# A fused attention, expert and gated feed-forward kernel: ScalarE makes the upper parts of all expert weights from block 6 on, and the experts' results are turned later

## The chip, the cores and the metric

The kernel runs on one core of a Trainium2 chip. The metric is the device time of one execution in microseconds (us). One execution was also taken with the hardware profiler; its rows are quoted below.

## The reference, cut to what matters

```python
# attention: 16 heads of 768 positions, 64 wide; a query sees the keys of its own hash bucket
scores = np.where(mask, scale * np.matmul(q, k.transpose(0, 1, 3, 2)), -1e9)
x = softmax(scores) @ v                      # as 1536 tokens x 512
# experts: 8, each token goes to one of them
h = np.maximum(xe @ w1[e], 0.0)              # w1[e]: 512 x 1024
out[mask] = gate_w[mask, None] * (h @ w2[e]) # w2[e]: 1024 x 512
# gated feed-forward on all 1536 tokens
xn = x / rms * rms_g
g = xn @ w_gate                              # 512 x 1536
return silu(g) * (xn @ w_val) @ w_out        # w_out: 1536 x 512
```

Everything is float32. The last layer's weights and scale arrive as 64-bit floats.

## The kernel before, in words

TensorE (PE) multiplies in its float32 matmul format, so every operand is held as two parts: `hi`, the value rounded to that format, and `lo`, the rest. A product is three matmuls: hi by hi, hi by lo and lo by hi. Three stages follow each other: attention (to about 265 us), the experts (265 to 453 us) and the gated feed-forward (453 us to the end). The order of each engine's instructions is written by hand, and every engine works through its own list in that order.

**Experts.** An expert has eight weight blocks of 128 x 1024, four of `w1` and four of `w2`; block `i` of the whole stage belongs to expert `i // 8`. Expert `e` runs four inner steps `f` over `w1` (24 matmuls into `ph`, then ScalarE's Relu to `hh` and VectorE's remainder `hl`) and four steps over `w2` (12 wider matmuls into the two banks `py`). At the head of each step `convert(i)` prepares a block that TensorE needs four steps later. The preparation has three parts:

- SP's queue loads the block into one of five `raw` tiles (L256).
- `split_piece` first calls `finish_split`, which issues the pass of VectorE (DVE) that makes `lo` of the block split before (L288) and then the load that reuses its `raw` tile. Then it issues the copy that makes `hi` of the new block: on GpSimd (POOL) for even blocks (L287), on ScalarE (ACT) for odd ones (L285).
- Six half blocks of the last layer's weights are converted in between by `split_half` (L325 to L334).

Blocks 0 to 5 are split during attention, on GpSimd alone. `flip_window(e + 1)` turns the next expert's tokens on TensorE in two groups of transposes. While expert `e` runs its first steps, `finish_rows` of expert `e - 1` scales its result on ScalarE and DVE (`y`, L205), and GpSimd scatters it to the memory table `yd` with two indirect transfers (L168).

**Hand-over.** The gated feed-forward needs all 1536 tokens as 12 turned tiles, four to a group `b`. `load_y(tt)` loads one from `yd` on SP's queue (L1132), into one of three buffers. `flip_y` makes four transposes into one of two PSUM banks `f`, copies the token numbers (`ids`) and `hi` (`gxh`, L1148) on ScalarE and makes `lo` (`gxl`, L1149) on DVE; then it asks for the tile three further on. `fillers` is a list of such generators, and `fill_pe` takes one step from it after each step of an expert. Before the change three loads stand at the end of the first product of expert 6, tiles 0 to 7 are turned after the eight steps of expert 7, and tiles 8 to 11 inside `glu(0, 1)`. A load of tiles 0 to 7 is declared free of the scatters of experts 6 and 7, but waits for those of experts 0 to 5; a load of tiles 8 to 11 waits for all.

**Gated feed-forward.** `glu(p_, b)` makes four groups of 12 matmuls (`pg`, `pv` twice), `project(p_, b)` four groups of six. Their order is glu(0,0), glu(0,1), project(0,0), glu(0,2), project(0,1) and so on.

Of the kernel before, what the change touches and what calls it, by code (L numbers as in the profile page):

```python
# [44 lines left out]
def turns(t):  # L45

    return t.rearrange("p (h a) -> p a h", h=2)
# [26 lines left out]
def lsh_attention_moe_glu(  # L74
# [15 lines left out]
    nc = tc.nc  # L90
# [185 lines left out]
    def split_piece():  # L276

        finish_split()
        i = at["piece"]
        at["piece"] += 1  # L280
        new_part(i, first[i][1], ring)
        hi, lo = parts[i][2:]
        r = raws.pop(0)
        if i % 2:
            nc.scalar.copy(hi, r)  # L285
        else:
            nc.gpsimd.tensor_scalar(hi, r, 1.0, 0.0, ALU.mult, ALU.add)  # L287
        pending.append((i, lambda: (nc.vector.tensor_tensor(lo, r, hi.bitcast(F32), ALU.subtract), load_next())))  # L288

    def split_early():  # L290
# [865 lines left out]
    with ExitStack() as mc:  # L1156
# [52 lines left out]
                    split_half()  # L1209

        done = iter(())
        for e in range(E):
            xh, xl = xT.pop(e)
            hid = []
            for f in range(NF):
                i = e * 2 * NF + f
                convert(i)
                wh, wl = part(i)[0:2]
                ph = ps_h.tile([P, 2, W], F32, tag="h", name=f"ph{e}{f}")
                for s_ in range(2):  # L1220
                    fs = slice(s_ * P, (s_ + 1) * P)
                    for c in range(KC):
                        nc.tensor.matmul(ph[:, s_], wh[:, c, fs], turns(xh[:, c]), start=c == 0, stop=False)  # L1223
                        nc.tensor.matmul(ph[:, s_], wh[:, c, fs], turns(xl[:, c]), start=False, stop=False)  # L1224
                        nc.tensor.matmul(ph[:, s_], wl[:, c, fs], turns(xh[:, c]), start=False, stop=c == KC - 1)  # L1225
                parts.pop(i)
                hh = mp.tile([P, 2, W], F32R, tag="hh", name=f"hh{e}{f}", bufs=6)
                hl = mp.tile([P, 2, W], F32R, tag="hl", name=f"hl{e}{f}", bufs=6)
                nc.scalar.activation(hh, ph, AF.Relu)
                nc.vector.scalar_tensor_tensor(hl, ph, 0.0, hh.bitcast(F32), ALU.max, ALU.subtract)  # L1230
                hid.append((hh, hl))
                next(done, None)
                if e == E - 2 and f == NF - 1:

                    for tt in range(YB):
                        load_y(tt)
                if f == (F0 if e == 0 else 1):
                    fillers.append(flip_window(e + 1))
                fill_pe()
            py = [ps_y.tile([P, DM], F32, tag="y", name=f"py{e}{j}") for j in range(2)]  # L1240
            for f in range(NF):
                i = e * 2 * NF + NF + f
                convert(i)
                wh, wl = part(i)[0:2]
                hh, hl = hid[f]
                for s_ in range(2):
                    fc = 2 * f + s_
                    for j in range(2):
                        js = slice(j * P, (j + 1) * P)
                        nc.tensor.matmul(py[j], hh[:, s_, js], turns(wh[:, s_]), start=fc == 0, stop=False)  # L1250
                        nc.tensor.matmul(py[j], hh[:, s_, js], turns(wl[:, s_]), start=False, stop=False)
                        nc.tensor.matmul(py[j], hl[:, s_, js], turns(wh[:, s_]), start=False, stop=fc == 2 * NF - 1)
                parts.pop(i)
                fill_pe()
            if e == E - 1:
                for f_ in fillers:
                    for _ in f_:
                        pass
            if e == E - 2:
                fillers.append(flip_y(0, (NBLK - 1) * TB))  # L1260
            done = finish(e, py)
        for _ in done:
            pass
        for tt in range((NBLK - 1) * TB, min(NT, (NBLK - 1) * TB + YB)):
            load_y(tt)


    with ExitStack() as gc:
# [9 lines left out]
        NP = F2 // W  # L1278
        freed = N1 + EARLY

        def glu(p_, b, filler):
            gh, gl = part(N1 + 3 * p_)[0:2]
            vh, vl = part(N1 + 3 * p_ + 1)[0:2]
            hi = rp.tile([P, 2, CW], F32R, tag="y2", name=f"hi{p_}{b}")
            lo = gp.tile([P, 2, CW], F32R, tag="lo2", name=f"lo{p_}{b}")
            for s_ in range(2):
                if p_ > 0 or b in GLU0:
                    split_half(freed + DEPTH)
                fs = slice(s_ * P, (s_ + 1) * P)
                pg = ps_g.tile([P, CW], F32, tag="g", name=f"pg{p_}{b}{s_}")  # L1290
                pv = ps_v.tile([P, CW], F32, tag="v", name=f"pv{p_}{b}{s_}")
                for ps_, wh, wl in ((pg, gh, gl), (pv, vh, vl)):
                    for c in range(KC):
                        nc.tensor.matmul(ps_, wh[:, c, fs], turns(xTh[b][:, c]), start=c == 0, stop=False)  # L1294
                        nc.tensor.matmul(ps_, wh[:, c, fs], turns(xTl[b][:, c]), start=False, stop=False)  # L1295
                        nc.tensor.matmul(ps_, wl[:, c, fs], turns(xTh[b][:, c]), start=False, stop=c == KC - 1)  # L1296
                sg = gp.tile([P, CW], F32, tag="sg", name=f"sg{p_}{b}{s_}")
                nc.scalar.activation(sg, pg, AF.Silu)
                nc.vector.tensor_tensor(sg, pv, sg, ALU.mult)  # L1299
                nc.scalar.copy(hi[:, s_], sg)  # L1300
                nc.vector.tensor_tensor(lo[:, s_], sg, hi[:, s_].bitcast(F32), ALU.subtract)
                for _ in range(2):
                    next(filler, None)
            hid[p_, b] = (hi, lo)

        def project(p_, b):
            oh_, ol_ = part(N1 + 3 * p_ + 2)[0:2]
            hi, lo = hid.pop((p_, b))
            for i in range(TB):
                tt = b * TB + i  # L1310
                ts_ = slice(i * P, (i + 1) * P)
                if i % 2 and p_ + b > 0:
                    z = ps_x.tile([P, DM], F32, tag="wx", name=f"z{p_}{tt}")
                else:
                    z = ps_z.tile([P, DM], F32, tag="z", name=f"z{p_}{tt}")
# [11 lines left out]
        last = None  # L1327
        for p_ in range(NP):
            for b in range(NBLK):
                filler = iter(())  # L1330
                if p_ == 0 and b == NBLK - 2:
                    filler = flip_y((NBLK - 1) * TB, NT)
                glu(p_, b, filler)
                for _ in filler:
                    pass
                if last is not None:
                    project(*last)
                    if last[1] == NBLK - 1:
                        for j in range(3):
                            parts.pop(N1 + 3 * last[0] + j)  # L1340
                        freed = max(N1 + EARLY, N1 + 3 * (last[0] + 1))
                last = (p_, b)
# [30 lines left out]
```

## Time and profile before

| what | value |
|---|---|
| time, median of 3 runs | 744.7 us (743.47 to 746.56) |
| the profiled execution: its time | 744.9 us |
| its span from first to last instruction | 742.9 us |
| TensorE busy | 720.8 us (97%) |
| VectorE (DVE) busy | 594.6 us (80%) |
| ScalarE (ACT) busy | 375.0 us (50%) |
| GpSimd (POOL) busy | 254.6 us (34%) |
| granted TensorE clock over the span | 0.998 |

A busy share is a mean over stages with different limits. TensorE's 97% means that its idle time is only some 22 us in all, so what counts is where these lie. A matmul's busy time contains its latency, so time that TensorE lost is also read from how far apart matmuls start.

### The profile page before, as it was taken

Reading aid. Unit: us, or ns where it says so; the run is one execution under the profiler, and the core shown is the slowest. Engines: PE = TensorE matmul, PEld = TensorE weight load, DVE = VectorE, ACT = ScalarE, POOL = GpSimd, SP = SyncE. Lnnn points to the kernel's source line nnn. Section 1 sums busy time; section 2 is a strip of 40 time slices with the busy share of each in tenths; the row PEclk is TensorE's granted clock in tenths of the full one; section 3 lists DMA queues with packets and bytes.
Section 4 is the critical chain, followed back from the end, with each engine's and each line's share of the span. In section 5 each row is a group of like instructions: output and inputs, shape, how many; then the busy total and the mean of one; then the engine's idle time right before and its main releaser. Section 6 shows DMA issues by size and latency. Waiting matters only on the chain.

```text
span 742.9 us, 12599 instructions
## 1 busy us (share of the span) xinstructions
PE 720.8 (97%) x4459; PEld 653.4 (88%) x4460; DVE 594.6 (80%) x1094; ACT 375.0 (50%) x777; POOL 254.6 (34%) x434
## 2 busy tenths in 40 slices
PE   8999999999999899999989999999999999999996
PEld 6898999999999899998989888888888888888885
DVE  5999999999999757888789967855877878778533
ACT  4898989998989535335453354433221221212210
POOL 4243344347645523325244333121121121211124
PEclk9999999999999999999999999999999999999999
DMA  6799956566651156777778585321122122210012
GB/s 164 175 250 249 235 138 158 140 153 176 175 129 37 51 176 203 232 213 242 246 219 263 151 288 160 117 86 58 56 80 63 56 82 62 69 45 1 0 58 113
DMA packets 80820, 103.45 MB, mean 139 GB/s; under 512 B 32072, under 2 KB 50504, under 8 KB 80753
## 3 DMA queue, kind: packets, MB, share of 16 engines
q1 hardware_dynamic: 76752, 92.95, 44.4%
q0 software_dynamic: 3200, 9.46, 3.4%
q8 instruction: 36, 0.59, 0.3%
q14 instruction: 32, 0.25, 0.1%
q10 hardware_dynamic: 800, 0.20, 0.1%
HBM read 69.53 MB, written 14.72 MB: 113 GB/s over the span
## 4 chain that ended last, share of the span: by engine, by line
PE 63%; DVE 15%; DMA 8%; issue 5%; ACT 4%; POOL 3%; SPq 2%; POOLq 0%; DVEq 0%; ACTq 0%
PE T L607 7%; DVE lo L288 5%; PE z L1317 4%; PE z L1319 4%; PE z L1318 4%; PE pv L1295 4%; PE pg L1295 4%; PE pg L1296 4%; PE pv L1296 4%; PE pg L1294 4%; PE pv L1294 4%; PE S L569 3%; PE O L639 3%; PE S L570 3%; PE O L641 3%
## 5 line engine op out<-in xcount | busy, mean ns | idle before, releaser
L333 POOL TENSOR_TENSOR wa<-wa,hi 128x512 f32<-128x512 f32 x36 | 58.1, 1613 | 215.9 <-ACT hi L329 209.5
L329 ACT CAST hi<-wa 128x512 fp32r<-128x512 f32 x36 | 22.3, 621 | 161.7 <-DVE wa L327 154.7
L588 ACT ACTIVATE P<-S,negm 128x768 f32<-128x768 f32 x96 | 95.8, 998 | 10.4 <-DVE negm L579 6.3
L617 DVE TENSOR_TENSOR ptl<-T,pth 128x384 fp32r<-128x384 f32 x192 | 97.3, 547 | 1.5 <-ACT pth L616 0.8
L574 DVE TENSOR_REDUCE neg<-S 128x1 f32<-128x768 f32 x96 | 90.8, 946 | 2.9 <-PE S L570 2.4
L616 ACT CAST pth<-T 128x384 fp32r<-128x384 f32 x192 | 83.2, 488 | 3.0 <-PE T L607 2.2
L288 DVE TENSOR_TENSOR lo<-raw,hi 128x1024 fp32r<-128x1024 f32 x58 | 83.3, 1470 | 1.6 <-POOL hi L287 1.6
L607 PE MATMUL T<-ident,P 128*128 128x128 f32 x576 | 81.5, 275 | 0.9 <-DVE ptl L617 0.5
L607 PEld LDWEIGHTS T<-ident,P 128*128 128x128 f32 x576 | 67.8, 141 | 7.0 <-DVE ptl L617 3.2
L569 PE MATMUL S<-kA,qA 76*128 76x384 f32 x192 | 66.2, 345 | 1.8 <-ACT P L588 0.9
L1225 PE MATMUL ph<-xTh,lo 128*128 128x256 f32 x224 | 61.7, 275 | 2.1 <-DVE lo L288 2.1
L570 PE MATMUL S<-kB,qB 128*128 128x384 f32 x192 | 63.0, 328 | 0.6 <-DMA qB<-kql 0.6
L1223 PE MATMUL ph<-xTh,hi 128*128 128x256 f32 x224 | 62.8, 280 | 0.0
L1224 PE MATMUL ph<-xTl,hi 128*128 128x256 f32 x224 | 61.6, 275 | 0.0
L639 PE MATMUL O<-ptl,vst 128*64 128x384 f32 (+1 forms) x198 | 59.8, 332 | 0.0
L1299 DVE TENSOR_TENSOR sg<-pv,sg 128x512 f32<-128x512 f32 x36 | 24.7, 687 | 40.9 <-PE pv L1296 40.9
L1294 PE MATMUL pg<-gxh,hi 128*128 128x512 f32 x144 | 54.7, 380 | 0.0
L1317 PE MATMUL z<-hi,hi 128*128 128x512 f32 x144 | 54.7, 380 | 0.0
L1295 PE MATMUL pg<-gxl,hi 128*128 128x512 f32 x144 | 54.6, 379 | 0.0
L1296 PE MATMUL pg<-gxh,lo 128*128 128x512 f32 x144 | 54.6, 379 | 0.0
L1294 PE MATMUL pv<-gxh,hi 128*128 128x512 f32 x144 | 54.6, 379 | 0.0
L1295 PE MATMUL pv<-gxl,hi 128*128 128x512 f32 x144 | 54.6, 379 | 0.0
(236 smaller groups left out, 1953.3 us busy)
## 6 DMA issues: line engine op xcount, KB each, us to landing
raw<-in_moe_w_dram SPq DMA_DIRECT2D x64, 512.0 KB
raw<-in_moe_w_gate_dram SPq DMA_DIRECT2D x12, 512.0 KB
raw<-in_moe_w_val_dram SPq DMA_DIRECT2D x12, 512.0 KB
raw<-in_moe_w_out_dram SPq DMA_DIRECT2D x12, 512.0 KB
xs<-fill SPq DMA_DIRECT2D x16, 257.0 KB
xw<-xs SPq DMA_DIRECT2D x7, 514.0 KB
yt<-yd SPq DMA_DIRECT2D x12, 256.5 KB
v<-in_v_dram SPq DMA_DIRECT2D x16, 192.0 KB
```

The lines of the kernel that those rows point to most:

```text
L288: pending.append((i, lambda: (nc.vector.tensor_tensor(lo, r, hi.bitcast(F32), ALU.subtract), load_next())))
L569: nc.tensor.matmul(s_[:, j, 0:HW], qA[n][:, t * P:(t + 1) * P], turns_by_tile(kA[n][:, cs]), start=True, stop=False)
L570: nc.tensor.matmul(s_[:, j, 0:HW], qB[n][:, t * P:(t + 1) * P], turns_by_tile(kB[n][:, cs]), start=False, stop=True)
L574: nc.vector.tensor_reduce(neg[u % 4][:, 1:2], St[u][:, :, 0:HW], AX.XY, ALU.max, negate=True)
L588: nc.scalar.activation(p_, St.pop(u)[:, :, 0:HW], AF.Exp, bias=nm[:, 1:2], scale=nm[:, 0:1], accum_out=sums[n][:, t:t + 1])
L607: nc.tensor.transpose(w[:, c * P:(c + 1) * P], p_[:, j, c * P:(c + 1) * P], ident)
L616: nc.scalar.copy(hi[:, 3 * j:3 * j + 3, cs], wv)
L617: nc.vector.tensor_tensor(lo[:, 3 * j:3 * j + 3, cs], wv, hi[:, 3 * j:3 * j + 3, cs].bitcast(F32), ALU.subtract)
L1294: nc.tensor.matmul(ps_, wh[:, c, fs], turns(xTh[b][:, c]), start=c == 0, stop=False)
L1295: nc.tensor.matmul(ps_, wh[:, c, fs], turns(xTl[b][:, c]), start=False, stop=False)
L1296: nc.tensor.matmul(ps_, wl[:, c, fs], turns(xTh[b][:, c]), start=False, stop=c == KC - 1)
L1317: nc.tensor.matmul(z, hi[:, s_, ts_], turns(oh_[:, s_]), start=s_ == 0, stop=False)
```

## The change

`split_piece` makes every `hi` on ScalarE; GpSimd's 29 copies are gone. The first three loads of the experts' results move from the end of the first product of expert 6 to the first step of expert 7. One generator turns all 12 tiles: tiles 0 to 4 at five places from the last `w1` step of expert 7 on, tiles 5 to 7 inside glu(0,0), tiles 8 to 11 inside project(0,0), each in front of one of its four groups.

```diff
         r = raws.pop(0)
-        if i % 2:
-            nc.scalar.copy(hi, r)
-        else:
-            nc.gpsimd.tensor_scalar(hi, r, 1.0, 0.0, ALU.mult, ALU.add)
+        nc.scalar.copy(hi, r)
         pending.append((i, lambda: (nc.vector.tensor_tensor(lo, r, hi.bitcast(F32), ALU.subtract), load_next())))
...
         done = iter(())
+        flips = flip_y(0, NT)
         for e in range(E):
...
-                if e == E - 2 and f == NF - 1:
+                if e == E - 1 and f == 0:
 
                     for tt in range(YB):
                         load_y(tt)
+                if e == E - 1 and f == NF - 1:
+                    fillers.append(flips)
...
-            if e == E - 1:
-                for f_ in fillers:
-                    for _ in f_:
-                        pass
-            if e == E - 2:
-                fillers.append(flip_y(0, (NBLK - 1) * TB))
...
-        for tt in range((NBLK - 1) * TB, min(NT, (NBLK - 1) * TB + YB)):
-            load_y(tt)
...
+        steps = 3
...
+                    if p_ + b == 0 and steps:
+                        steps -= 1
+                        next(flips)
...
-                for _ in range(2):
-                    next(filler, None)
...
+                if p_ + b == 0:
+                    next(flips)
...
-                filler = iter(())
-                if p_ == 0 and b == NBLK - 2:
-                    filler = flip_y((NBLK - 1) * TB, NT)
-                glu(p_, b, filler)
-                for _ in filler:
-                    pass
+                glu(p_, b)
```

ScalarE's list in the first product of expert 3, before the change and with it. `hi28` is the upper part of weight block 28, `hh31` the Relu of expert 3's step 1, `y2` and `py20` belong to the finish of expert 2, and `xTh4` is the next expert's tokens.

```order
L285 CAST hi27_5414<-raw29_5345 128x1024
L1229 ACTIVATE hh30_5460<-ph30_5435 128x512
L189 ACTIVATE y2_5464<-py20_5342,xw2_4668 128x512
L189 ACTIVATE y2_5464<-py21_5343,xw2_4668 128x512
L193 ACTIVATE py20_5342,yst2_5465<-y2_5464 128x512
L193 ACTIVATE py21_5343,yst2_5465<-y2_5464 128x512
L285 CAST hi29_5475<-raw31_5381 128x1024
L1229 ACTIVATE hh31_5503<-ph31_5478 128x512
L197 ACTIVATE yst2_5465<-yst2_5465 128x2
L1185 CAST xTh4_5509<-wxw40_5511 128x512
L1229 ACTIVATE hh32_5549<-ph32_5524 128x512
```

```order
L284 CAST hi27_5414<-raw29_5345 128x1024
L284 CAST hi28_5432<-raw30_5363 128x1024
L1227 ACTIVATE hh30_5460<-ph30_5435 128x512
L189 ACTIVATE y2_5464<-py20_5342,xw2_4668 128x512
L189 ACTIVATE y2_5464<-py21_5343,xw2_4668 128x512
L193 ACTIVATE py20_5342,yst2_5465<-y2_5464 128x512
L193 ACTIVATE py21_5343,yst2_5465<-y2_5464 128x512
L284 CAST hi29_5475<-raw31_5381 128x1024
L1227 ACTIVATE hh31_5503<-ph31_5478 128x512
L197 ACTIVATE yst2_5465<-yst2_5465 128x2
L1182 CAST xTh4_5509<-wxw40_5511 128x512
L284 CAST hi30_5521<-raw32_5387 128x1024
```

The copies of blocks 28 and 30 have come into ScalarE's list, each ahead of a Relu.

GpSimd's list over the same stretch, before the change: the copies of even blocks stand around the two scatters of expert 2's result.

```order
L287 TENSOR_SCALAR hi30_5521<-raw32_5387 128x1024
L167 MEMSET mark_81 1x8
L168 DMA yd_80<-y2_5464,posw_85 1536x513
L167 MEMSET mark_81 1x8
L168 DMA yd_80<-y2_5464,posw_85 1536x513
L287 TENSOR_SCALAR hi32_5617<-raw34_5430 128x1024
L287 TENSOR_SCALAR hi34_5653<-raw36_5519 128x1024
```

With the change only the scatters and the small memsets and copies are left of these rows.

DVE's list at the hand-over, before and after. `gxl1<-f7` is the lower part of turned tile 7, `y7` the scaled result of expert 7, `sg000` the first gate product of glu(0,0).

```order
L1149 TENSOR_TENSOR gxl1_4650<-f7_6800,gxh1_4648 128x8x64
L196 TENSOR_SCALAR yst7_6809<-yst7_6809 128x2
...
L205 SCALAR_TENSOR_TENSOR y7_6808<-y7_6808,yst7_6809,rg_78 128x512 x2
L1299 TENSOR_TENSOR sg000_6888<-pv000_6863,sg000_6888 128x512
L1301 TENSOR_TENSOR lo00_6861<-sg000_6888,hi00_6860 128x512
L1299 TENSOR_TENSOR sg001_6919<-pv001_6894,sg001_6919 128x512
```

```order
L1146 TENSOR_TENSOR gxl1_4650<-f4_6774,gxh1_4648 128x8x64
L196 TENSOR_SCALAR yst7_6785<-yst7_6785 128x2
...
L205 SCALAR_TENSOR_TENSOR y7_6784<-y7_6784,yst7_6785,rg_78 128x512 x2
L1146 TENSOR_TENSOR gxl1_4650<-f5_6846,gxh1_4648 128x8x64
L1146 TENSOR_TENSOR gxl1_4650<-f6_6868,gxh1_4648 128x8x64
L1298 TENSOR_TENSOR sg000_6878<-pv000_6833,sg000_6878 128x512
L1300 TENSOR_TENSOR lo00_6831<-sg000_6878,hi00_6830 128x512
L1146 TENSOR_TENSOR gxl1_4650<-f7_6897,gxh1_4648 128x8x64
```

The passes of tiles 5 to 7 have moved from ahead of `y7` to behind it, among the products of glu(0,0).

## Rows read from the trace of the kernel before

**Rows 1.** The page's head: the profiled execution's span.

```profile
span 742.9 us, 12599 instructions
```

**Rows 2.** Timeline of PE: first matmuls of experts 1 to 7 and of glu(0,0).

```profile
start us, us, engine line op out<-in xcount [idle before <-releaser]
287.23 0.27 PE L1223 MATMUL ph<-xTh,hi 128*128 128x256 f32 x1
...
309.57 0.27 PE L1223 MATMUL ph<-xTh,hi 128*128 128x256 f32 x1
...
331.52 0.27 PE L1223 MATMUL ph<-xTh,hi 128*128 128x256 f32 x1
...
355.47 0.27 PE L1223 MATMUL ph<-xTh,hi 128*128 128x256 f32 x1
...
377.43 0.27 PE L1223 MATMUL ph<-xTh,hi 128*128 128x256 f32 x1
...
401.74 0.27 PE L1223 MATMUL ph<-xTh,hi 128*128 128x256 f32 x1
...
424.95 0.27 PE L1223 MATMUL ph<-xTh,hi 128*128 128x256 f32 x1
...
453.23 0.46 PE L1294 MATMUL pg<-gxh,hi 128*128 128x512 f32 x1
```

**Rows 3.** Waits of PE from 300 us on: us in total, times, longest.

```profile
PE py L1251 <- DVE lo L288: 2.5, 3, 1.2
PE f L1143 <- DMA yt<-yd: 2.3, 3, 1.2
PE ph L1225 <- DVE lo L288: 2.1, 1, 2.1
PE f L1143 <- DVE gxl L1149: 0.8, 1, 0.8
```

**Rows 4.** L288 on DVE: the page's group, then ns min/median/max from its source view.

```profile
L288 DVE TENSOR_TENSOR lo<-raw,hi 128x1024 fp32r<-128x1024 f32 x58 | 83.3, 1470 | 1.6 <-POOL hi L287 1.6
...
L288 DVE TENSOR_TENSOR lo<-raw,hi x58: 1210/1214/3522, 274.7 to 447.3; 128x1024 fp32r<-128x1024 f32 x58
```

**Rows 5.** Timelines in expert 3: POOL, DVE and PE around 349 us.

```profile
347.31 1.03 POOL L168 DMA_INDIRECT yd<-y,posw  x1 [7.32 <-DVE y L205]
...
348.65 1.11 POOL L168 DMA_INDIRECT yd<-y,posw  x1 [0.21 <-issue]
349.79 2.06 POOL L287 TENSOR_SCALAR hi<-raw 128x1024 fp32r<-128x1024 f32 x2
...
349.43 3.50 DVE L288 TENSOR_TENSOR lo<-raw,hi 128x1024 fp32r<-128x1024 f32 x1
...
352.99 0.48 PE L1251 MATMUL py<-lo,hh 128*128 128x512 f32 x1 [1.17 <-DVE lo L288]
```

**Rows 6.** Source views of L287 and L285: durations (ns), and L287's longest wait.

```profile
L287 POOL TENSOR_SCALAR hi<-raw x29: 1036/1057/2165, 268.0 to 435.0; 128x1024 fp32r<-128x1024 f32 x29
...
  DMA raw<-in_moe_w_dram: 34.0, 7
...
L285 ACT CAST hi<-raw x29: 1037/1052/1102, 273.9 to 437.9; 128x1024 fp32r<-128x1024 f32 x29
```

**Rows 7.** Windows over expert 4's two halves: PE, PEld, DVE, ACT, POOL, clock, DMA.

```profile
355.47:367.06 11.59, 11.59 (x105) 11.59 (x104) 7.29 (x12) 7.01 (x14) 2.39 (x5) 1.00 0.76 265
367.06:377.43 10.37, 10.37 (x51) 9.08 (x50) 10.16 (x15) 1.45 (x3) 3.45 (x5) 1.00 0.85 235
```

**Rows 8.** Waits of SP's queue: its loads of the experts' results.

```profile
SPq L1132 <- DMA yd<-y,posw: 16.0, 2, 9.9
```

**Rows 9.** Timelines at the hand-over: PE's second group, DVE's last `y`; then L1149's mean.

```profile
455.90 0.38 PE L1294 MATMUL pv<-gxh,hi 128*128 128x512 f32 x1
...
459.63 1.42 DVE L205 SCALAR_TENSOR_TENSOR y<-y,yst,rg 128x512 f32<-128x512 f32 x2
...
L1149 DVE TENSOR_TENSOR gxl<-f,gxh 128x512 fp32r<-128x512 f32 x12 | 8.0, 686 | 4.6 <-ACT gxh L1148 4.6
```

More of the change, by code (lines that the diff above doesn't have):

```diff
@@ L1279, in lsh_attention_moe_glu, with glu @@
         freed = N1 + EARLY
-        def glu(p_, b, filler):
+        steps = 3
+        def glu(p_, b):
+            nonlocal steps
             gh, gl = part(N1 + 3 * p_)[0:2]
```

## Prediction

> **What bounds the kernel now.** I read first where TensorE starts each expert, since its busy share hides lost time inside overlapping matmuls. The starts stand 21.95 us apart where nothing disturbs it (experts 2 and 4: 331.52 - 309.57 and 377.43 - 355.47 = 21.96). The other gaps are 22.34, 23.95, 24.31 and 23.21 us [rows 2]. Experts 1 to 6 together take 424.95 - 287.23 = 137.72 us, and six undisturbed ones would take 131.7: 6.0 us are lost there. TensorE is the bound of this stage, and what it waits for is named by the waits: 2.5 + 2.1 = 4.6 us on VectorE's `lo` of expert weights. The other 3.1 us are waits of the tile turns: 2.3 on the loads of `yt` and 0.8 on a PSUM bank that `gxl` gives back [rows 3]. Idle time counts a stall short, because the latency of the matmul before it covers a part: 4.6 us of idle time stand for 6.0 lost, so I put the turns at 3.1 x 6.0 / 4.6 = 4.1 us lost. Together 10.1 us are to be had, and no more by this route.
>
> The second view says why `lo` is late. The pass takes 1.21 us at the median and 3.52 at the longest, and its mean is 1.47, so the 58 passes carry 58 x (1470 - 1214) ns = 14.8 us of something else [rows 4]. The timelines of expert 3 show it: GpSimd holds back in front of the scatters (7.32 us) until VectorE has `y`, issues the second scatter, and then makes two copies of even blocks back to back from 349.79 to 351.85. VectorE's pass of 349.43 lasts 3.50 us and ends 1.1 us after these copies; TensorE, which needs this `lo` in the last step of expert 3, starts again at 352.99, 1.17 us late [rows 5]. The held pass is that of block 31. Its upper part is an odd one, which ScalarE made, so it isn't its own input that it waits for: it stands still while GpSimd copies.
>
> By the Trainium skill, "SBUF — State Buffer", the section "SBUF: two separate sides", VectorE and GpSimd share one pair of ports as an exclusive lock: a VectorE operation with two SBUF inputs and a GpSimd operation that reads SBUF exclude each other, and the loser is blocked for the whole of one instruction. The trace agrees on the exclusion but not on the size: the pass of block 31 was held for two copies, 3.50 - 1.21 = 2.29 us, and it had started first. By the page's one copy of about 1.06 us the recovered time of the first term below would be 5.5 x 1.06 / 2.29 = 2.5 us, and the sum 740.6 us; I go by the row.
>
> **The copies.** Removed: 29 copies on GpSimd, 1.057 us each at the median. Added: 29 on ScalarE, where the same copy takes 1.052 us [rows 6], so 30.5 us of ScalarE time over the stage. None of it is on the path by itself: in an undisturbed expert ScalarE is busy for 7.01 of the 11.59 us of the first product and 1.45 of the 10.37 us of the second [rows 7]. Two more copies in the first product make 7.01 + 2.1 = 9.1 us, two or three in the second 1.45 + 3.2 = 4.6. Both fit. What they can do is push: each copy stands ahead of a Relu or a finish step, so VectorE may get `hh`, `xTh` and the sums for `y` up to 2.1 us later. VectorE is busy for 7.29 of 11.59 us there [rows 7], so it has 4.3 us in which to take that push.
>
> What the term gives has two ends. In expert 3 the pass of block 31 would start at 349.43 and take 1.21 us: it ends at 350.64, and TensorE asked for it at 352.99 - 1.17 = 351.82. So if VectorE takes the push, nothing of the loss is left: 6.0 us. If the whole push of 2.1 us arrives, the pass ends at 352.74, and 0.9 us stay lost in each of six experts: 6.0 - 5.4 = 0.6 us. By the 4.3 us of room the first end is nearer; I take 5.5 us, with 0.5 left. Loads of raw blocks follow `lo` on SP's queue, so they go out earlier by what VectorE is no longer held; that is not counted apart.
>
> **The loads and turns.** The number of instructions is the same, 12 loads and 48 transposes, so only waits move. Three loads at the end of expert 6's first product hold SP's queue for the scatter of expert 5: of 16.0 us in two waits the shorter is 16.0 - 9.9 = 6.1 [rows 8], and the raw loads behind it stand still. At the first step of expert 7 that scatter has landed, and the wait should be gone. In expert 7 the first turn comes four steps after its load, and each later load has three turns' distance, a step of 2.6 to 2.9 us each with the turn between. The waits of 2.3 us for `yt` should go.
>
> New waits come from the banks and from VectorE's order. Turn 7 needs the bank of turn 5, whose `gxl` now stands behind `y` of expert 7. Today `y` ends at 461.05, that is 7.8 us after glu(0,0) starts at 453.23, and a `gxl` takes 0.69 us [rows 9]: the bank would be free at 8.5 us. A group of 12 matmuls takes 455.90 - 453.23 = 2.67 us, so turn 7, after three groups and two turns of some 0.4 us, asks at 8.8. That fits by 0.3 us. If `y` comes later, because the two weight halves that VectorE converts in the last steps of expert 7 start later against the turns, it costs up to what it is late; bounds 0 and 2 us, and I take 1.2. Turn 11 stands in front of the last group of project(0,0), which is half as long as a group of glu, 1.3 us, and glu(0,2) needs its `gxl` at once; ScalarE's copy and VectorE's pass, some 0.7 us each with a hand-over between, end 0.3 to 1 us too late. I take 0.7. With 0.4 us for the `gxl` that glu(0,0) and glu(0,1) start on, 2.3 us are lost instead of 4.1: a gain of 1.8, with ends of 0.3 and 3.7.
>
> The second wait of SP, 9.9 us for the last expert's scatter, stays: three loads now stand in glu(0,0) and wait. Turn 8 comes only after glu(0,1), eight groups or 21 us after the start, so this is hidden by the products; without that cover it would cost its 9.9 us.
>
> **The sum.** Profiled execution 744.9 us (span 742.9 [rows 1] and 2.0 around it): 744.9 - 5.5 - 1.8 = 737.6. This execution lies 0.2 us above the median of the runs, 744.7, which I neglect. The waits of TensorE reach to the end of the program and name none behind the hand-over but those of the turns [rows 3], so what is won before it comes off the end.
>
> **The rivals.**
>
> *ScalarE becomes the late engine.* Its list in the first product gets a copy ahead of nearly every Relu, and the copy must wait for its raw block in order. For it: at the end of the first product, where VectorE's `lo` decides, a push of only 1.2 us uses up the margin of 351.82 - 350.64. Against it: 9.1 us of work in 11.59. Then the first term shrinks to its lower end, 0.6: with half of the turns' gain, 744.9 - 0.6 - 0.9 = 743.4.
>
> *The change doesn't do what it seems to: the loads are the bound.* Then `lo` is late because the raw block is, and another engine for the copy changes nothing; for it speak GpSimd's waits on raw blocks, 34.0 us in seven [rows 6]. Against it: in an undisturbed expert the DMA engines are busy for 0.76 x 11.59 + 0.85 x 10.37 = 17.6 of 21.96 us [rows 7], and in expert 3 the pass that was late had its raw block and its upper part. Only the turns' 1.8 us stay: 743.1.
>
> *Slower: raw blocks hold ScalarE, and with it the Relu.* GpSimd's seven waits of 34.0 / 7 = 4.9 us on the average [rows 6] move to ScalarE's queue, and behind each stands a Relu, `y` or `xTh`. TensorE asks for the bank of the first step again in the fourth, two steps or 5.8 us (half of 11.59) after the first ends. From there it decides: a wait that delays Relu and `hl` by more than that stops TensorE. If blocks came 2.6 us later than GpSimd saw them, 7.5 us each, experts 1 to 7 would lose 1.7 us each: 744.9 + 7 x 1.7 - 1.8 = 755.0. Against it: the loads go out earlier, not later, and the waits that GpSimd shows began when it had nothing else to do.
>
> **How the numbers follow.** Chances: my sum 0.74, ScalarE late 0.13, loads the bound 0.07, ScalarE held 0.06. My case with both terms at their ends runs from 744.9 - 6.0 - 3.7 = 735.2 to some 741.5; the range takes in the whole 10.1 us (734.8) and the two cases near 743.4 at the upper end: 734.8 to 743.4. That leaves out the slower case and small parts at both ends. A difference of 0.5% (3.7 us) is about what a measurement of this kernel can tell from none: faster is below 741.0. My case lies there but for 0.02 and the second and third reach there with 0.03: faster 0.75, same 0.19 (0.17 of the second and third, 0.02 of mine), slower 0.06.
>
> **What would show it.** Right: the passes of VectorE that make `lo` of a block all near 1.21 us, with a mean under 1.25; experts 1 to 6 each 21.95 to 22.5 us apart; no wait of SP for `yd` near the start of expert 7; ScalarE at about 405 us busy and GpSimd at about 224. Wrong: TensorE waiting for `lo` as often as now while its passes are short (then ScalarE or the loads are late), long waits of ScalarE on raw blocks with Relu behind them, or turns of tiles 5 to 11 that wait more than 4 us in all. The prediction fails most easily on the 2.29 us: if the pass at 349.43 stood still for another reason than GpSimd's copies, nothing of the first term comes.

## The result, and the profile after

The changed kernel takes 737.25 us, the median of six runs (735.7 to 739.31), against 744.48 us for the kernel before, timed beside it: a ratio of 0.990, with a 95% interval of 0.989 to 0.992. The profile's head shows the span 7.1 us shorter than in [rows 1]; TensorE's busy time is nearly the same (720.2 us after 720.8), so its share is larger.

```profile
span 735.8 us, 12536 instructions
...
PE 720.2 (98%) x4459; PEld 653.4 (89%) x4460; DVE 576.9 (78%) x1094; ACT 402.1 (55%) x806; POOL 223.2 (30%) x405
```

Start with TensorE's timeline, as in [rows 2]: the first matmuls of experts 1 to 7, the one turn that waits long, and the start of glu(0,0).

```profile
286.70 0.27 PE L1221 MATMUL ph<-xTh,hi 128*128 128x256 f32 x1
...
308.65 0.27 PE L1221 MATMUL ph<-xTh,hi 128*128 128x256 f32 x1
...
330.61 0.27 PE L1221 MATMUL ph<-xTh,hi 128*128 128x256 f32 x1
...
352.74 0.27 PE L1221 MATMUL ph<-xTh,hi 128*128 128x256 f32 x1
...
374.70 0.27 PE L1221 MATMUL ph<-xTh,hi 128*128 128x256 f32 x1
...
396.77 0.27 PE L1221 MATMUL ph<-xTh,hi 128*128 128x256 f32 x1
...
418.96 0.27 PE L1221 MATMUL ph<-xTh,hi 128*128 128x256 f32 x1
...
441.74 0.63 PE L1140 MATMUL f<-ident,yt 128*128 128x128 f32 x4 [2.81 <-DMA yt<-yd]
...
445.16 0.46 PE L1290 MATMUL pg<-gxh,hi 128*128 128x512 f32 x1
```

Experts 1 to 6 take 418.96 - 286.70 = 132.26 us where they took 137.72; against six times 21.95 they lose 0.6 us instead of 6.0. From the start of expert 7 to the start of glu(0,2) it is 55.88 us (418.96 to 474.84) instead of 56.82 (424.95 to 481.77). These two stretches, called the experts and the hand-over below, changed by 5.46 and 0.94 us. What follows glu(0,2) is as long as before (261.0 against 261.2 us), and expert 1 starts 0.5 us earlier than in [rows 2].

The source views of the two lines that prepare a block (the columns are ns min/median/max, then first and last start) and ScalarE's waits for raw blocks answer [rows 4] and [rows 6].

```profile
L285 DVE TENSOR_TENSOR lo<-raw,hi x58: 1209/1216/1226, 274.4 to 437.6; 128x1024 fp32r<-128x1024 f32 x58
...
L284 ACT CAST hi<-raw x58: 1030/1050/1076, 272.2 to 430.0; 128x1024 fp32r<-128x1024 f32 x58
...
  DMA raw<-in_moe_w_dram: 24.2, 8
```

The longest of VectorE's 58 passes fell from 3.52 to 1.23 us. The windows over the two halves of expert 4 answer [rows 7]; the fourth busy time is ScalarE's.

```profile
352.74:364.34 11.60, 11.60 (x106) 11.60 (x105) 5.85 (x9) 9.13 (x17) 0.00 (x0) 1.00 0.76 258
364.34:374.70 10.36, 10.36 (x51) 9.07 (x50) 9.96 (x18) 3.67 (x5) 2.96 (x4) 1.00 0.81 237
```

TensorE's waits from 300 us on answer [rows 3]: no wait of its matmuls for a `lo` is left, only turns.

```profile
PE f L1140 <- DMA yt<-yd: 3.1, 2, 2.8
```

SP's waits answer [rows 8]: the 6.1 us wait near the start of expert 7 is gone, the long one stays.

```profile
SPq L1129 <- DMA yd<-y,posw: 9.2, 1, 9.2
```

The new wait of 2.81 us is read in SP's timeline and in VectorE's.

```profile
429.62 5.10 SPq L256 DMA_DIRECT2D raw<-in_moe_w_gate_dram  x2
434.88 1.85 SPq L1129 DMA_DIRECT2D yt<-yd  x3
...
433.05 1.22 DVE L285 TENSOR_TENSOR lo<-raw,hi 128x1024 fp32r<-128x1024 f32 x1
```

The second of the two raw loads needs the `raw` tile that VectorE's pass of 433.05 frees, and this pass stands behind `y` of expert 6. The load of tile 3 stands behind that raw load on SP's queue, goes out at 434.88 and lands at about 441.6.

### The profile page after: what moved, and what is told of

It reads as the page before. It is cut to its first block, busy times and chain, and to the rows that moved or that the text cites. A ratio compares the mean times of both kernels' runs of the same rounds, so it can differ in the third digit from the quotient of the medians.

```text
span 735.8 us, 12536 instructions
## 1 busy us (share of the span) xinstructions
PE 720.2 (98%) x4459; PEld 653.4 (89%) x4460; DVE 576.9 (78%) x1094; ACT 402.1 (55%) x806; POOL 223.2 (30%) x405
## 4 chain that ended last, share of the span: by engine, by line
PE 50%; DMA 4%; ACT 3%; issue 3%; DVE 2%; POOL 2%; SPq 0%; POOLq 0%; ACTq 0%; DVEq 0%
PE pg L1291 4%; PE pv L1292 4%; PE pv L1291 4%; PE pg L1292 4%; PE pv L1290 4%; PE pg L1290 4%; PE z L1317 3%; PE z L1318 3%; PE z L1316 3%; PE ph L1221 3%; PE ph L1223 3%; PE ph L1222 3%; PE py L1251 2%; PE py L1250 2%; PE py L1252 2%
## 5 line engine op out<-in xcount | busy, mean ns | idle before, releaser
L585 ACT ACTIVATE P<-S,negm 128x768 f32<-128x768 f32 x96 | 95.8, 998 | 10.1 <-DVE negm L576 6.5
L285 DVE TENSOR_TENSOR lo<-raw,hi 128x1024 fp32r<-128x1024 f32 x58 | 68.7, 1216 | 6.5 <-ACT hi L284 6.5
L284 ACT CAST hi<-raw 128x1024 fp32r<-128x1024 f32 x58 | 60.0, 1054 | 24.9 <-DMA raw<-in_moe_w_dram 24.2
L1316 PE MATMUL z<-hi,hi 128*128 128x512 f32 x144 | 54.9, 381 | 0.0
L1292 PE MATMUL pg<-gxh,lo 128*128 128x512 f32 x144 | 54.6, 379 | 0.0
```

The lines of the kernel that those rows point to most:

```text
L585: nc.scalar.activation(p_, St.pop(u)[:, :, 0:HW], AF.Exp, bias=nm[:, 1:2], scale=nm[:, 0:1], accum_out=sums[n][:, t:t + 1])
L1316: nc.tensor.matmul(z, hi[:, s_, ts_], turns(oh_[:, s_]), start=s_ == 0, stop=False)
```

## The experiments

Two theories stood against each other. H: VectorE's passes are held while GpSimd copies. L: the upper parts of the blocks whose copies stand behind a scatter come late. (In the expectations of stuck_half and free_half, Theory A is L and Theory B is H.) Each run was timed beside the kernel before, and the ratio is to that time: 744.14 us for copies_only to pool_writes, 745.42 for free_half, stuck_half, loads_early and turn_earlier, 744.65 for the other four. "Lost" is what experts 1 to 6 take above 131.7 us, read from TensorE's timeline of the profiled execution. An asterisk marks a stretch in which the granted clock fell to 0.50 behind a pause of TensorE.

| run | time, us | ratio to before, interval | lost, us | hand-over, us | mean of a `lo` pass, ns |
|---|---|---|---|---|---|
| before | | | 6.0 | 56.8 | 1470 |
| the change | 737.25 | 0.990 (0.989 to 0.992) | 0.6 | 55.9 | 1216 |
| copies_only | 742.69 | 0.997 (0.996 to 0.999) | 0.0 | 61.2* | 1216 |
| turns_only | 742.10 | 0.997 (0.995 to 0.999) | 7.1* | 54.2 | 1480 |
| pool_reads | 738.02 | 0.992 (0.990 to 0.994) | 1.7 | 54.0 | 1369 |
| pool_writes | 735.69 | 0.988 (0.986 to 0.990) | 0.1 | 55.0 | 1216 |
| free_half | 735.87 | 0.988 (0.986 to 0.990) | 0.0 | 54.3 | 1294 |
| stuck_half | 744.18 | 0.999 (0.997 to 1.001) | 7.9* | 56.9* | 1435 |
| hold_only | 741.83 | 0.997 (0.996 to 0.998) | 4.8* | 54.2 | 1420 |
| late_only | 736.51 | 0.989 (0.988 to 0.991) | 0.0 | 54.6 | 1218 |
| loads_early | 742.15 | 0.996 (0.995 to 0.998) | 0.0 | 59.1* | 1218 |
| turn_earlier | 737.04 | 0.989 (0.987 to 0.991) | 0.0 | 54.9 | 1218 |
| act_extra | 748.07 | 1.005 (1.003 to 1.007) | 10.1* | 56.1 | 1218 |
| spread | 738.13 | 0.993 (0.991 to 0.995) | 0.0 | 57.3* | 1289 |

Whether such a fall comes in every execution of a kernel isn't shown, so it is taken off where two profiled executions are compared. By the windows (time multiplied by one minus the granted clock) each costs some 1.7 us, in copies_only 2.4. Without them the experts lose an estimated 5.4 us in turns_only, 6.2 in stuck_half, 3.1 in hold_only and 8.4 in act_extra, and the hand-over takes 58.8 us in copies_only, 55.2 in stuck_half, 57.4 in loads_early and 55.6 in spread. The profiled executions of the kernel before and of the change have no such fall in these stretches.

### Each part alone

**copies_only**: the copies go to ScalarE, loads and turns stay as before. This is its edit against the kernel before; the other edits below are against the changed kernel.

```diff
-        if i % 2:
-            nc.scalar.copy(hi, r)
-        else:
-            nc.gpsimd.tensor_scalar(hi, r, 1.0, 0.0, ALU.mult, ALU.add)
+        nc.scalar.copy(hi, r)
```

> The copies of even blocks go to ScalarE, the loads and turns of the experts' results stay where they were. If VectorE's late passes came from GpSimd's copies (held by them, or fed late by them), all passes that make lo take about 1.21 us, experts 1 to 6 stand 21.95 to 22.2 us apart, and the time falls by 5 to 6 us to about 739; the turns keep their 4.1 us. If the measured gain came from the turns instead, this one stays within 1 us of 744.5.

The experts lose nothing, which is 6.0 us won, but the time of about 739 us didn't come: the hand-over takes 61.2 us, 4.3 more than before. Its timelines of ScalarE and PE, its SP waits and its windows around 433 us (PE's busy time comes first, the granted clock stands after GpSimd's) show where that goes.

```profile
427.75 1.05 ACT L284 CAST hi<-raw 128x1024 fp32r<-128x1024 f32 x1 [6.31 <-DMA raw<-in_moe_w_dram]
...
433.02 1.12 PE L1140 MATMUL f<-ident,yt 128*128 128x128 f32 x4 [3.05 <-DVE gxl L1146]
```

```profile
SPq L1129 <- DMA yd<-y,posw: 15.2, 2, 10.2
```

```profile
430.00:433.00 3.00, 0.00 (x0) 0.00 (x0) 0.75 (x3) 3.00 (x8) 0.00 (x0) 0.84 0.62 236
433.00:436.00 3.00, 2.98 (x14) 2.99 (x15) 2.16 (x4) 1.88 (x6) 0.00 (x0) 0.50 0.51 151
```

SP waits 15.2 - 10.2 = 5.0 us for a scatter with raw loads behind it, ScalarE waits 6.31 us for a raw block with a Relu and a turn's `gxh` behind it, and TensorE stops for 3.05 us. From within this pause on the granted clock is 0.50, the lower level (1.2 GHz): the next 24 matmuls take 5.19 us where 24 take 2.76 elsewhere, another 2.4 us.

**turns_only**: loads and turns as in the change, even copies on GpSimd.

```diff
-        nc.scalar.copy(hi, r)
+        if i % 2:
+            nc.scalar.copy(hi, r)
+        else:
+            nc.gpsimd.tensor_scalar(hi, r, 1.0, 0.0, ALU.mult, ALU.add)
```

> The loads and turns move, the copies of even blocks stay on GpSimd. By the prediction's second term the gain is 1.8 us; by the profile of the changed kernel, in which the turns still lost 3.4 us, it is about 1 us: 743.5. Passes of 3.5 us stay in every expert. If copies and turns help each other, this one gains nothing.

The hand-over falls by 2.6 us to 54.2. The experts still lose 7.1 us; with the fall of the clock in expert 5 taken off that is 5.4, near the 6.0 of the kernel before. The two parts alone give 1.5 and 2.0 us on the medians, together 7.2, so they don't add up. The copies need the other part, without which the hand-over gets longer. That the loads and turns need the copies isn't shown: their own stretch gained more here than in the change.

### What holds TensorE in the experts

**stuck_half** and **free_half**: only two of an expert's four even blocks go back to GpSimd, those behind the scatters or the other two.

```diff
-        nc.scalar.copy(hi, r)
+        if i % 2 or i % 8 in (4, 6):      # free_half: in (0, 2)
+            nc.scalar.copy(hi, r)
+        else:
+            nc.gpsimd.tensor_scalar(hi, r, 1.0, 0.0, ALU.mult, ALU.add)
```

> The mirror image: the two even blocks of an expert whose copies stand behind the scatters (index 0 and 2) go back to GpSimd, the other two stay on ScalarE. Theory A (lateness behind the scatter): nearly all of the 4.9 us between the changed kernel and the one that moved only the loads and turns come back: experts 1 to 6 lose 4 us or more and the time is 741 to 742 us. Theory B (held passes): half, as with the other half, about 740 us, and the mean of the lo passes is about 1.35 us. If this kernel and its mirror image both stay at 737 to 738 us, it takes all four copies together, and neither theory holds alone.

> The changed kernel, but of the four even blocks of an expert the two whose copies do not stand behind a scatter (blocks with index 4 and 6 in the expert) go back to GpSimd; the two behind the scatters stay on ScalarE. Theory A, the loss of the kernel before came mainly from copies that start late because they stand behind a scatter on GpSimd's queue: nearly all of the gain stays, experts 1 to 6 lose at most 1.5 us against six times 21.95, and the time is 737 to 739 us, although VectorE's passes that make lo have some long ones again (mean about 1.35 us). Theory B, the loss came from VectorE's passes being held while GpSimd reads SBUF: half of the copies give half of the loss back, some 3 us, and the time is about 740 us. In both the move of the loads and turns is as in the changed kernel.

All of the loss hangs on the two copies behind the scatters (7.9 us lost against 0.0). That was what L expected, though both times lie outside its ranges. But the timelines of stuck_half in expert 3 show no late upper part: VectorE goes through five passes without a pause, and they take 8.05 us where four take 4.62 in the changed kernel, so a fifth would make some 5.8. Nowhere in experts 1 to 6 do the waits of stuck_half list one of VectorE for an upper part. The source view has the longest pass.

```profile
350.08 2.08 POOL L287 TENSOR_SCALAR hi<-raw 128x1024 fp32r<-128x1024 f32 x2
...
349.73 8.05 DVE L288 TENSOR_TENSOR lo<-raw,hi 128x1024 fp32r<-128x1024 f32 x5
...
353.30 0.48 PE L1254 MATMUL py<-lo,hh 128*128 128x512 f32 x1 [1.17 <-DVE lo L288]
```

```profile
L288 DVE TENSOR_TENSOR lo<-raw,hi x58: 1209/1215/3519, 274.1 to 444.6; 128x1024 fp32r<-128x1024 f32 x58
```

So the two theories were taken apart. **hold_only** gives back the copies without the lateness: every upper part is ScalarE's, and GpSimd copies something that nobody waits for. **late_only** gives back the lateness without a read: VectorE's pass waits for a GpSimd memset behind the scatters.

```diff
         nc.scalar.copy(hi, r)
+        if i % 8 in (0, 2):                                   # hold_only
+            nc.gpsimd.tensor_scalar(room[0][:, 0:2], fill[:, None, 0:DM].to_broadcast([P, 2, DM]), 1.0, 0.0, ALU.mult, ALU.add)
...
+        if i % 8 in (0, 2):                                   # late_only
+            for _ in range(2):
+                nc.gpsimd.memset(fill[:, 0:DM], 0.0)
+            nc.gpsimd.memset(lo.bitcast(F32)[:, 0:8], 0.0)
```

> The changed kernel (every upper part by ScalarE), with one extra GpSimd copy of 128x1024 from a constant tile into a tile that is not in use then, behind each scatter pair, at the two places of an expert where the kernel with the stuck copies had its own. Nothing waits for these copies; they read SBUF and that is all they do. The output is unchanged. Theory H, what costs the time behind the scatters is that VectorE's passes stand still while GpSimd copies: six or so passes of 3.5 us are back, experts 1 to 6 lose 5 us or more, and the time is 741 to 744 us. Theory L, what costs it is that the upper parts come late there: passes may be held, but experts 1 to 6 stay within 2 us of six times 21.95, and the time is 736 to 738 us.

> The counterpart: the changed kernel, with two GpSimd memsets of 128x512 (about 1.06 us together) and one of the first eight columns of the block's lower part at the same two places behind the scatters. VectorE's pass must wait for that small memset as it had to wait for the stuck copy, but a memset reads nothing. The output is unchanged. Theory H (held passes): the passes stay at 1.21 us, experts 1 to 6 stay within 1 us of six times 21.95, and the time is 735.5 to 737.5 us. Theory L (lateness): experts 1 to 6 lose 5 us or more, 741 to 744 us. If both this kernel and its counterpart are fast, it takes both together.

hold_only loses 4.8 us in the experts, late_only nothing. Timelines of hold_only in expert 3 and at TensorE's one long wait, and its source view:

```profile
348.10 3.04 POOL L287 TENSOR_SCALAR gxh<-fill 128x1024 fp32r<-128x1024 f32 x2
...
347.74 7.89 DVE L288 TENSOR_TENSOR lo<-raw,hi 128x1024 fp32r<-128x1024 f32 x5
...
380.16 0.38 PE L1227 MATMUL ph<-xTh,lo 128*128 128x256 f32 x1 [2.20 <-DVE lo L288]
```

```profile
L288 DVE TENSOR_TENSOR lo<-raw,hi x58: 1207/1215/2511, 274.1 to 441.5; 128x1024 fp32r<-128x1024 f32 x58
```

In late_only's timeline VectorE does wait for GpSimd, but 0.32 us, and its passes keep their length:

```profile
350.57 3.50 DVE L289 TENSOR_TENSOR lo<-raw,hi 128x1024 fp32r<-128x1024 f32 x3 [0.32 <-POOL lo L288]
```

Not all of the 4.8 us are waits. Behind the one of 2.20 us the granted clock fell, as these windows of hold_only show:

```profile
380.10:383.00 2.90, 2.84 (x16) 2.85 (x17) 2.90 (x5) 2.90 (x7) 0.08 (x2) 0.62 0.55 172
383.00:386.00 3.00, 3.00 (x23) 3.00 (x23) 1.87 (x3) 1.01 (x3) 0.00 (x0) 0.80 0.79 254
```

The same fall is in stuck_half, so the two are compared without it: a hold alone costs an estimated 3.1 us, half of stuck_half's 6.2, and the lateness that late_only makes costs none. H stands, but not in the size that it expected (5 us or more, passes of 3.5 us). Of the 3.0 us between hold_only and stuck_half 2.0 lie in expert 3: stuck_half loses 2.5 us there and hold_only 0.6. In stuck_half both copies hold one pass, for 3.51 us, and VectorE starts it 18.5 us into the expert; in hold_only it lasts 2.50 us, held by little more than one copy takes, and VectorE starts it at 17.5 us. Why the copies hold less there, and whether lateness adds to a hold, wasn't tried.

**pool_reads** and **pool_writes** add GpSimd work at the same two places to the changed kernel, two copies of 128x512 from a constant tile onto itself, or two memsets of it; the output is unchanged.

```diff
+        if i % 8 in (0, 2):
+            for _ in range(2):
+                nc.gpsimd.tensor_scalar(fill[:, 0:DM], fill[:, 0:DM], 1.0, 0.0, ALU.mult, ALU.add)
+                # pool_writes: nc.gpsimd.memset(fill[:, 0:DM], 0.0)
```

> The changed kernel, and for each block 8e and 8e+2 (the two whose copies stood behind the scatters) GpSimd makes two copies of a 128 x 512 constant tile onto itself, which nobody waits for. If GpSimd's copies hold VectorE's passes by themselves, the pass behind each pair of scatters lasts 3 us or more again, experts 3, 5 and 6 lose some 2 us each and the time is 740 to 742. If VectorE was late because its upper parts came late from GpSimd's list, nothing changes: 737.3.

> The same, but GpSimd only writes zeros into that tile and reads nothing. If only operations of GpSimd that read SBUF shut out a VectorE pass with two SBUF inputs, all passes stay at 1.21 us and the time at 737.3. If any work of GpSimd in SBUF does, passes of over 2 us come back and the time is 739 or more.

The source views of pool_reads and of pool_writes:

```profile
L288 DVE TENSOR_TENSOR lo<-raw,hi x58: 1208/1220/1639, 275.5 to 440.0; 128x1024 fp32r<-128x1024 f32 x58
...
L287 POOL TENSOR_SCALAR fill<-fill x28: 619/1470/1537, 267.2 to 421.0; 128x512 f32<-128x512 f32 x28
```

```profile
L288 DVE TENSOR_TENSOR lo<-raw,hi x58: 1211/1215/1226, 274.0 to 436.9; 128x1024 fp32r<-128x1024 f32 x58
...
L287 POOL MEMSET fill<- x28: 524/529/568, 265.7 to 415.7; 128x512 f32 x28
```

GpSimd's reads stretch VectorE's passes, its writes don't, although the passes of 3 us or more and the 740 us that a hold was expected to bring back in pool_reads didn't come. With short copies it is mostly GpSimd that stands still (1470 ns at the median, 619 at the least), and no pass is longer than 1.64 us. The 58 x (1369 - 1216) ns = 8.9 us that the passes are stretched cost TensorE 1.7 us, all in expert 5.

### Loads, turns and room on ScalarE

**loads_early**: the changed kernel with the first three loads at the end of expert 6's first product again.

```diff
-                if e == E - 1 and f == 0:
+                if e == E - 2 and f == NF - 1:
```

> The changed kernel, but the first three loads of the experts' results are issued at the end of expert 6's first product again; the turns stay where the change put them. Theory A, what the kernel with the copies alone lost at expert 7 (4.3 us) came from SP's wait for the scatter with raw loads behind it: SP waits about 6 us near the start of expert 7, ScalarE waits 4 us or more for a raw block with a Relu behind it, TensorE stops by 2 to 3 us in expert 7, and the time is about 740 us. Theory B, it came from the places of the turns: SP's wait is back, but with the turns late nothing on TensorE follows from it, and the time is 736 to 738 us; the 2.8 us that the fourth turn waits for its tile may even vanish, since its load is asked for as before.

Theory A: SP's wait is back, and so is ScalarE's for the raw block behind it, and the hand-over takes 59.1 us. Its SP waits, ScalarE's timeline and a window (granted clock after GpSimd's busy time):

```profile
SPq L1129 <- DMA yd<-y,posw: 14.1, 2, 9.3
```

```profile
425.14 1.05 ACT L284 CAST hi<-raw 128x1024 fp32r<-128x1024 f32 x1 [6.01 <-DMA raw<-in_moe_w_dram]
```

```profile
438.00:441.00 3.00, 2.61 (x9) 2.25 (x10) 2.05 (x4) 0.59 (x1) 1.09 (x3) 0.62 0.85 197
```

TensorE waits 0.71 us for a late `hl`, 1.92 and 1.23 us at two turns, and behind the second of these waits the clock falls. Of the 3.2 us by which the hand-over is longer than the change's, some 1.7 are this fall. What matters is when ScalarE's wait ends. At the start of expert 7 it waits 5.7 us in the change and 5.3 us in loads_early, and that stops nothing; the wait of 6.01 us is a second one, which ends 6.6 us into the expert.

**turn_earlier**: the first turn one step of expert 7 earlier, so that the load of tile 3 goes onto SP's queue ahead of the raw load.

```diff
-                if e == E - 1 and f == NF - 1:
+                if e == E - 1 and f == NF - 2:
...
-        steps = 3
+        steps = 2
```

> The changed kernel, but the first turn comes one step of expert 7 earlier, so all turns up to the fifth move up by one step and two instead of three are left for glu(0,0)'s groups. The load of the fourth tile then goes onto SP's queue ahead of the load of raw block 71, which in the changed kernel waits for VectorE and made that tile 2.8 us late. Theory A (the queue order makes the fourth tile late): this wait goes, nothing takes its place, and the time is 734.5 to 735.5 us, 0.997 of the changed kernel. Theory B (the tile is late because its transfer runs against the scatter of expert 6): the tile lands as late as before, the wait stays or grows by the step that its turn moved up, and the time is 737 to 739 us.

Its timelines of SP and PE:

```profile
430.12 0.33 SPq L1129 DMA_DIRECT2D yt<-yd  x1
434.81 0.38 SPq L256 DMA_DIRECT2D raw<-in_moe_w_gate_dram  x1
...
441.74 0.63 PE L1140 MATMUL f<-ident,yt 128*128 128x128 f32 x4 [0.86 <-DMA yt<-yd]
```

The load went out 5.6 us earlier, counted from the start of expert 7, and the wait of 2.81 us went with it, so the order on SP's queue made that tile late. But something did take its place, waits of 0.5 to 0.9 us at three turns. The hand-over gained 1.0 us, too little to show in the ratios (0.989 against 0.990), and the time of 734.5 to 735.5 us was missed.

**act_extra**: the changed kernel with a second copy on ScalarE behind each even block's.

```diff
         nc.scalar.copy(hi, r)
+        if i % 2 == 0:
+            nc.scalar.copy(room[0][:, 0:2], fill[:, None, 0:DM].to_broadcast([P, 2, DM]))
```

> The changed kernel with a second copy of 128x1024 on ScalarE (from a constant tile into a tile that is not in use then) behind each even block's upper part, so that the work that the change moved to ScalarE is there twice, some 29 us more. The output is unchanged. It tells how much room ScalarE has. If ScalarE is near its limit in the first product (9.1 of 11.59 us by the prediction's estimate, 11.2 with this): experts 1 to 6 lose 3 us or more and the time is above 740 us. If it has room: within 1 us of the changed kernel, 736 to 738 us.

Slower than the kernel before, with 10.1 us lost in the experts, some 1.7 of them to a fall of the clock behind the wait of 2.45 us. Its PE waits in the experts, and its window over the first half of expert 4:

```profile
PE py L1255 <- DVE lo L288: 6.2, 5, 2.4
```

```profile
358.14:369.80 11.66, 11.66 (x106) 11.65 (x105) 4.86 (x8) 9.07 (x16) 0.00 (x0) 1.00 0.80 271
```

ScalarE is busy for no more of this half than in the changed kernel; the work spilled into the second half. What is late is the order: each extra copy pushes a Relu, VectorE waits for it with `hl` (22.5 us in 18 waits over experts 1 to 6, where it was 13.4 in nine), and the next `lo` stands behind that.

**spread** was put together as a faster version: free_half's copies, turn_earlier's start, and turn 8 moved into glu(0,1).

```diff
+                    if p_ == 0 and b == 1 and s_ == 1 and ps_ is pg:
+                        next(flips)
...
-                if p_ + b == 0:
+                if p_ + b == 0 and i < TB - 1:
                     next(flips)
```

> A version put together from what the runs showed: the blocks behind the scatters and the odd ones on ScalarE, blocks 4 and 6 of an expert on GpSimd; the first turn one step of expert 7 earlier, turns 6 and 7 in glu(0,0), turn 8 inside glu(0,1) behind its third group, and turns 9 to 11 in front of the first three groups of project(0,0), so that the last has two groups behind it before glu(0,2). If the small waits of the turns (0.8 us for a bank, 0.4 us for a tile, some 0.7 us lost around them) go by this, the stretch from expert 7 to glu(0,2) falls from 54.3 us to about 53, and the time is 734 to 735 us. If a turn inside glu(0,1) waits for the last scatter instead, the stretch stays at 54 us or above and the time at 736 us.

It came out slower than either case: 738.13 us, with 57.3 us for the stretch. Its timelines of SP and PE show the last tile's load behind a raw load again, 4.2 us ahead of its turn, and its window behind that turn a granted clock of 0.54, so some 1.7 us of the stretch are clock:

```profile
466.00 0.38 SPq L256 DMA_DIRECT2D raw<-in_moe_w_gate_dram  x1
466.56 0.34 SPq L1132 DMA_DIRECT2D yt<-yd  x1
...
470.77 0.68 PE L1143 MATMUL f<-ident,yt 128*128 128x128 f32 x4 [2.17 <-DMA yt<-yd]
```

```profile
471.00:474.00 3.00, 3.00 (x11) 2.46 (x10) 1.90 (x4) 0.58 (x1) 0.00 (x0) 0.54 0.00 0
```

free_half (735.87 us) is the fastest that computes the same with no added work, but its interval overlaps that of the changed kernel.

## Why the prediction was right, point by point

**The bound and the loss.** Right: experts 1 to 6 went from 6.0 us lost to 0.6. The 0.6 left need not be ScalarE's push, since copies_only with the same copies loses 0.0.

**The copies, 5.5 us.** The term measured 5.46 us. Its mechanism, passes that stand still while GpSimd copies, is shown by hold_only against late_only for about half of the loss; for the rest the trace of stuck_half shows held passes and no wait for an upper part, but no run sets a hold of that length alone. The prediction laid it on all 29 copies; free_half shows that the 15 that stay on GpSimd there cost nothing, although they hold passes for 58 x (1294 - 1216) ns = 4.5 us. In these traces the held passes that cost time are those behind `y` and the scatters, where VectorE has a run of work and TensorE waits for its end; in expert 5 that run goes on through the conversion of a weight half. Of the Trainium skill's rule ("SBUF — State Buffer", section "SBUF: two separate sides") the runs agree with the side condition that only a GpSimd operation that reads SBUF excludes VectorE's pass: 1369 ns on the average beside copies, 1216 beside memsets. On its size, the loser blocked for one instruction, they differ: in hold_only the longest pass is 1.3 us over the median, beside one copy of 1.06 us, but in stuck_half it is 2.3 us over it, beside two copies of 2.08 us together.

**ScalarE's room.** 9.1 us of work were foretold for the first product of expert 4, and 9.13 measured; 4.6 for the second, and 3.67. The conclusion held, but "4.3 us in which to take that push" was no margin to build on: the same number of copies once more cost 10.1 us (8.4 without the fall of the clock). A sign that the prediction had named for being wrong did appear, long waits of ScalarE on raw blocks with a Relu behind them: 24.2 us in eight. They ended early enough and stopped nothing on TensorE.

**The loads and turns, 1.8 us.** In the profiled execution this term was mis-sized: 0.94 us. The step that failed is "each later load has three turns' distance" with its conclusion, "The waits of 2.3 us for `yt` should go." Distance in turns doesn't say when a load starts: tile 3's stood behind a raw load that waits for VectorE. The foretold new waits, 1.2 us for turn 7's bank and 0.7 for turn 11, did not come as waits of TensorE; one of 2.81 us came in their place. SP's two waits went as foretold: the shorter vanished, the longer stayed at 9.2 us and was hidden. How large the term is stays open, since it is read from one execution. In six other kernels with the same loads and turns (turns_only, pool_reads, pool_writes, free_half, hold_only, late_only) the hand-over takes 54.0 to 55.0 us, 1.9 to 2.8 less than before; in act_extra, where one turn waits 2.99 us, it takes 56.1. The ends that the prediction gave this term, 0.3 and 3.7 us, aren't what its own pieces add up to, 0.7 and 3.4.

**The sum.** 737.6 us against 737.25. That it came out so close is in part luck. From one profiled execution to the other, 744.9 to 737.5 us, the two stretches give 6.4 of the 7.4 us; the other 1.0 lies outside them, where the prediction put nothing. Half of it is the earlier start of expert 1, which varies between these kernels from 286.4 to 289.4 us. With both of its terms at their lower ends, 0.6 and 0.3, the prediction's case reaches 744.0; the 741.5 that it names isn't worked out. The total was right, but that it is a sum was not: the moved loads carry more than their term. Without them ScalarE, in place of GpSimd, waits 6 us for a raw block with the Relu behind it. That is the mechanism of the third rival; it was set aside because "the loads go out earlier, not later", and that holds only with both parts together. copies_only shows its price, 4.3 us in the hand-over, of which 2.4 are clock. loads_early, where the turns stay late, has a hand-over 3.2 us longer than the change, of which some 1.7 are clock.

**The rivals.** ScalarE was not late, but the same copies once more make it so. The loads were not the bound: copies_only loses nothing in the experts.

## What to carry to other kernels

Before you move a copy off a shared path, find the moment at which the engine that it holds has a run of work that something waits for; copies at other times can stay. On an engine that works in order, ask of each moved instruction what it waits for and what stands behind it, since a wait that was harmless on an idle engine may stop the bound one on a busy engine. Time two parts alone as well as together: here 1.5 and 2.0 us became 7.2.

## What the runs showed of the hardware

A pause of TensorE can cost twice. Windows over stuck_half, behind a wait of 1.85 us in expert 5 (granted clock after GpSimd's busy time):

```profile
382.60:385.00 2.40, 2.35 (x16) 2.36 (x17) 2.40 (x3) 2.40 (x6) 0.07 (x2) 0.75 0.53 157
385.00:388.00 3.00, 3.00 (x19) 3.00 (x19) 2.23 (x4) 1.94 (x4) 0.00 (x0) 0.63 0.89 274
```

The same place in the kernel before, behind a wait of 2.10 us:

```profile
384.00:387.00 3.00, 3.00 (x29) 3.00 (x28) 3.00 (x4) 0.82 (x2) 0.58 (x1) 1.00 0.91 296
```

With the clock at 1.00 that expert lost 24.31 - 21.95 = 2.4 us, with the fall 25.71 - 21.95 = 3.8. From expert 1 to glu(0,2) the runs here have twelve pauses of 1.85 us or more. Eight brought a fall (1.85 and 1.93 us in stuck_half, 1.92 in loads_early, 2.08 in turns_only, 2.17 in spread, 2.20 in hold_only, 2.45 in act_extra, 3.05 in copies_only) and four brought none (1.86 in pool_writes, 2.10 in the kernel before, 2.81 in the change, 2.99 in act_extra). So the length of the pause alone doesn't decide; what does wasn't tried. turns_only has the copies of the kernel before and nearly its pause at this place, with a fall, so a loss read from one trace need not be that of every execution.
